# Fourteen zero stores cut from 128 rows to 120, and one more of 112 rows

## The chip, the cores and the metric

The kernel runs on one core of a Trainium2 chip. The metric is the device time of one execution in microseconds (us). The core has a tensor engine (PE, with its weight loads shown as PEld), a vector engine (DVE), a scalar engine (ACT), GpSimd (POOL) and a sync engine (SP). Here SP issues nearly all transfers between the chip's memory (DRAM) and the on-chip memory (SBUF, 128 rows called partitions). The transfers are carried by 16 DMA engines, which the profile counts together.

## The reference

A decoder of four layers runs forward and backward for a single token of 1,024 numbers: attention, MLP, attention, MLP, both times with the same weights. Cut to what matters:

```python
def A(x, k_cache, v_cache, wq, wo):          # attention over the last W = 4096 keys of 32768
    q = x @ wq                               # 32 heads of 128
    k, v = k_cache[:, :, Sk - W:], v_cache[:, :, Sk - W:]    # 4 groups
    p = softmax(q @ k.T * Dh ** -0.5)
    return (p @ v) @ wo
def B(x, w1, b1, w2):                        # 1024 -> 3584 -> 1024
    h = x @ w1 + b1
    return (h * tanh(softplus(h))) @ w2
x = x + A(norm(x), ...); x = x + B(norm(x), ...); x = x + A(norm(x), ...); x = x + B(norm(x), ...)
out, vjp = jax.vjp(f, x, k_cache, v_cache, wq, wo, w1, b1, w2)
return out, *vjp(grad_out)
```

The outputs are the result and the gradients of all eight inputs in bfloat16. The gradients of `k_cache` and `v_cache` have the caches' full size, 4 groups x 32,768 keys x 128; only the last 4,096 keys of each group were read, so the first 28,672 rows of each group are zero. Writing these zeros is part of the result: 8 areas of 7.3 MB, 58.7 MB out of the 168 MB that the SP queue moves.

## The kernel before

All matrices pass through SBUF in tiles of 128 partitions. The forward and backward pass work layer by layer: attention forward (`attn_fwd`, layer A1), the MLP forward with a first part of its backward (`mlp_B2_fwd`), attention again (A3), the last MLP forward and backward (`mlp_B4`), then `attn_bwd` for A3, `mlp_B2_bwd`, and `attn_bwd` for A1. The last part makes the weight gradients, which are outer products: `run_jobs` goes through a list of jobs (w2, then w1 mixed with the K and V gradients, then wo and wq), each of which multiplies on PE, moves the product from PSUM to SBUF with ACT or DVE (L890 and L893), and stores it.

The order of the work is written out by hand; there is no scheduler. SP issues its transfers strictly in program order. The transfers rotate over eight completion semaphores (101 to 106, 109 and 110), so that a transfer is issued only when the one eight before it has landed. Loads of weights stand in a list, `queue`, and `pump` (L182, L190, L199, L201) issues the next one when its slot of a ring is given back.

The zeros are cut into 112 jobs, `zero_jobs`: two outputs x 4 groups x 14 pieces. An area is seen as 128 rows of 57,344 bytes (`zflat`), and a piece is 2,048 elements of every row, so 128 x 4,096 bytes. `zeros(n)` takes the next n jobs and issues a store for each (two adjoining ones go in one store where the source has 4,096 elements). The source changes over the program: `zlo`, 1,024 elements read twice (L149); `zt`, 2,048 elements (L151); at the end `z8`, 4,096 elements (L151). Calls of `zeros` are spread over the whole program: in `attn_fwd` by the list `Z_`, in `mlp_B4` by `ZB4` after each block, in `attn_bwd`, in `mlp_B2_bwd`, and from `out_step` and `run_jobs` on beside the outer products. There is no wait for a zero store other than the semaphore rotation and the reuse of its source.

The names that matter below: `zero_jobs`, `zeros`, `zsrc` (the present source and its width), `Z_`, `ZB4`, `run_jobs`, and `add("w2", ...)`, whose last argument is the number of zero stores that follow a job of w2.

Of the kernel before, what the change touches and what calls it, by code (L numbers as in the profile page):

```python
# [17 lines left out]
G = 4  # L18
# [3 lines left out]
def kernel(  # L22
# [22 lines left out]
    nc = tc.nc  # L45
# [8 lines left out]
    ZR = Sk - W  # L54
# [33 lines left out]
    sB, sA, zlo, zt = misc[:, 0:1024], misc[:, 1024:2048], misc[:, 2048:3072], misc[:, 1024:3072]  # L88
# [42 lines left out]
    zero_jobs = []  # L131
    per = ZR // P * DH
    for out_t in (out_2, out_3):
        for g in range(G):
            zflat = out_t[0, g, 0:ZR, :].rearrange("(p r) d -> p (r d)", p=P)
            for i in range(per // 2048):
                zero_jobs.append((zflat, i))
    zsrc = [None, 1024]

    def zeros(n, after=None):  # L140
        while n > 0 and zero_jobs:
            zf, i = zero_jobs.pop(0)
            k = 1
            if zsrc[1] == 4096 and n > 1 and zero_jobs and zero_jobs[0][1] == i + 1 and i % 2 == 0:
                zero_jobs.pop(0)
                k = 2
            dst = zf[:, i * 2048:(i + k) * 2048]
            if zsrc[1] == 1024:
                d = nc.sync.dma_start(dst.rearrange("p (a b) -> p a b", a=2), zlo[:, None, :].to_broadcast([P, 2, 1024]))  # L149
            else:  # L150
                d = nc.sync.dma_start(dst, zsrc[0][:, 0:k * 2048])  # L151
            gate(d, after)
            after = None
            n -= k
# [301 lines left out]
    def attn_fwd(x_col, l, first, p_dst, F_, Z_):  # L456
        sv, n_bf, g0 = ln_fwd(x_col, l)
        if first:
            constants()
        zeros(Z_[0])  # L460
        big = two_banks()
        for t in range(TD):
            for n in range(8):
# [73 lines left out]
        nc.vector.tensor_copy(operm[:], pps[:])  # L537
        o32 = kt([P, HQ], FP32, f"o32_{l}")
        nc.vector.tensor_copy(o32[:], acc[:])
        zeros(Z_[2])  # L540
        sv["o32"], sv["p"] = o32, p_dst
        fill(F_[4])
        R = one_tile("R", 512)
# [84 lines left out]
            nc.vector.tensor_mul(d3[:, 1, :], dps[:], m3[:, 1, :])  # L628

    def mlp_B2_fwd(x_col):  # L630
        zeros(3)
        sv, n_bf, g0 = ln_fwd(x_col, "B2")
        hacc = one_tile("acc", TF)
        for i in range(16):
            t, hf = i // 2, i % 2
            w, ring, sl = take(("w1h", i))
            for b in range(NW2):
                fb = hf * NW2 + b
                o = (b // 2) * 2 * P + b % 2
                mm(hacc[:, fb:fb + 1], w[:, o:o + 2 * P - 1:2], n_bf[:, t:t + 1], i == 0 and b == 0, t == TD - 1)  # L640
            rel(ring, sl)
            if i == 1:
                bcast_g(gpair[:, LI["B4"], :])
        zeros(1)
        h = wk("h", TF)
        nc.vector.tensor_add(h[:], hacc[:], b1_f[:])
        dact = kt([P, TF], FP32, "dact_B2")
        mish(h[:], apair[:, 1, :], dact[:], TF)
        sv["dact"] = dact
        R, dps, ds = w2_pass(apair[:, 1, :], gpair[:, LI["B4"], :], {8: 1, 9: 1, 10: 1, 11: 1})  # L650
        nc.gpsimd.memset(sA, 0.0)
        zsrc[:] = [zt, 2048]
        da4 = kt([P, TF], FP32, "da4")
        y = d_cols(R)
        x_new = kt([P, TD], FP32, "x_B2")
        nc.vector.tensor_add(x_new[:], x_col[:], y[:])
        da_merge(da4[:], dps, ds)
        return x_new, sv, da4

    def mlp_B4(x_col, da4):  # L660
        sv, n_bf, g0 = ln_fwd(x_col, "B4", 2)
        dh = kt([P, TF], FP32, "dh_B4")
        sv["dh"] = dh
        R = one_tile("R", 512)
        big = two_banks()
        blk, hcol = {}, {}

        def fwd(b):
            full = b < 3
            nh, nt, nch = (2, 2, 4) if full else (1, 4, 2)  # L670
            hb = big[b % 2]
            blk[b] = [take(("w1b", b, i)) for i in range(nch)]
            for i in range(nch):
                fill(FT4[b][i])
                w = blk[b][i][0]
                for ti in range(nt):
                    t = nt * i + ti
                    for n in range(nh):
                        g = 2 * n + ti if full else ti
                        mm(hb[32 * g:32 * g + 32, :], bc(n_bf[:, t:t + 1]), w[:, ti, n * 512:(n + 1) * 512],  # L680
                           i == 0, i == nch - 1, tile_position=(0, 32 * g))
            evac(jkf[:, :], hb[:], 512, "D")

        def sel(b):
            full = b < 3
            nh, nk = (2, 8) if full else (1, 4)
            hps = sm_tile(P, 8)
            for cc in range(2):
                for tt in range(2):
                    k = 2 * cc + tt  # L690
                    mm(hps[:, k:k + 4 * (nh - 1) + 1:4], jkf[:, cc * 256 + tt:cc * 256 + tt + 255:2], selD[:] if full else sel1[:], k == 0, k == 3)
            h = wk("h", nk)
            nc.vector.tensor_add(h[:], hps[:, 0:nk], b1_f[:, 8 * b:8 * b + nk])
            hcol[b] = h

        def act(b):
            nk, f0 = 8 if b < 3 else 4, 8 * b
            dact = wk("dact", nk)
            mish(hcol[b][:], apair[:, 0, f0:f0 + nk], dact[:], nk)
            nc.vector.tensor_mul(hpair[:, 0, f0:f0 + nk], da4[:, f0:f0 + nk], dact[:])  # L700
            nc.vector.tensor_mul(dh[:, f0:f0 + nk], da4[:, f0:f0 + nk], dact[:])
            spent(2.8, 0.2)

        def turn(b, lo, hi):
            for u in range(lo, hi):
                if b < 3:
                    w = blk[b][u // 2][0][:, u % 2, :]
                    T8([w[:, (k // 2) * 256 + k % 2:(k // 2) * 256 + k % 2 + 255:2] for k in range(8)], w)
                else:
                    w = blk[b][u // 2][0][:, 2 * (u % 2):2 * (u % 2) + 2, :]  # L710
                    T8([w[:, q, (k // 2) * 256 + k % 2:(k // 2) * 256 + k % 2 + 255:2] for q in range(2) for k in range(4)],
                       w.rearrange("p t f -> p (t f)"))

        def bwd(b):
            nk, f0 = 8 if b < 3 else 4, 8 * b
            for k in range(nk):
                for tp in range(4):
                    w = blk[b][tp][0][:, 0:2, :] if b < 3 else blk[b][tp // 2][0][:, 2 * (tp % 2):2 * (tp % 2) + 2, :]
                    mm(R[32 * tp:32 * tp + 32, 0:256].rearrange("p (t d) -> p t d", t=2), bc(hpair[:, 0, f0 + k:f0 + k + 1]),
                       w[:, :, k * P:(k + 1) * P], b == 0 and k == 0, b == 3 and k == nk - 1, tile_position=(0, 32 * tp))  # L720
            for _, ring, i in blk.pop(b):
                rel(ring, i)

        for b in range(4):
            fwd(b)
            fill(FB4[b][0])
            sel(b)
            act(b)
            turn(b, 0, 8 if b < 3 else 4)
            fill(FB4[b][1])  # L730
            bwd(b)
            if b == 3:
                zsrc[:] = [None, 1024]
            zeros(ZB4[b])
        evac(jkf[:, 0:256], R[:, 0:256], 256, "D")
        dn = sm_tile(P, TD)
        for i in range(2):
            mm(dn[:].rearrange("p (a i) -> p i a", i=2)[:, i, :], jkf[:, i * P:(i + 1) * P], ident_f[:, 0:P:32], i == 0, i == 1)
        tt = wk("xx", 2 * TD)
        nc.vector.tensor_copy(tt[:, 0:TD], dn[:])  # L740
        return tt, sv

    def attn_bwd(g_col, g_bf, l, sv, last, nxt, F_, Z_, step):
# [9 lines left out]
            nc.gpsimd.dma_start(wo[:, 0, :], p3_d[:])  # L753
        else:
            p_t, ds_t = sv["p"], sA
        zeros(Z_[0])
        acc = one_tile("acc", HQ)
        j_cols(big, acc, 8, F_[0], True)
        do32 = wk("do32", HQ)
# [32 lines left out]
            rings["rb"] += range(2, 8)  # L792
            pump()
        nc.scalar.activation(dqpair[:, LI[l], :], qacc[:], ACT.Copy, scale=scale)
        zeros(Z_[2])
        step(3)
        fill_kind("wq")
        R = one_tile("R", 512)
# [229 lines left out]
    def wo_dead():  # L1028
# [32 lines left out]
        after = []  # L1061
# [9 lines left out]

        for n in range(NW2 // 2):
            add("w2a", n, lambda c=2 * n: pair_half(row_sp["w2"], c, w2_out, w2_lhs, 0))
            add("w2", n, lambda c=2 * n: pair_half(row_sp["w2"], c, w2_out, w2_lhs, 1), 1)
        for n in range(16):
            add("w1", n, lambda t=n // 2, hf=n % 2: w1_job(t, hf))
            add("kv", n, lambda n=n: kv_step(n))
# [5 lines left out]
    def run_jobs(n):  # L1083
        while jobs and (n > 0 or not jobs[0][0]):
            job, f, z = jobs.pop(0)
            f()
            zeros(z)
            n -= job

    def kv_step(i):  # L1090
# [13 lines left out]
    def out_step(i):  # L1104
        if i == 0:
            nc.scalar.copy(z8.bitcast(FP32), zlo[:, 0:2].bitcast(FP32).to_broadcast([P, 2048]))
            zsrc[:] = [z8, 4096]
            zeros(8)
        elif i < 3:
            rows_turn(row_sp["w2"], i - 1, w2_sp[i - 1], "rep")  # L1110
        elif i > 2:
            run_jobs(1 if i == 4 else 2)

    ZB4 = [11, 11, 10, 8]
    FT4 = [(0, 0, 0, 0), (6, 2, 2, 2), (6, 2, 2, 2), (8, 3)]
    FB4 = [(1, 0), (1, 0), (1, 0), (1, 2)]

# [5 lines left out]
    g3, g3b, _ = ln_bwd(tt, sB4, gcol, "A3", nfill=2)  # L1123
    g2, g2b, _ = attn_bwd(g3, g3b, "A3", sA3, False, "B2", [4, 3, 5, 2], [5, 1, 5], lambda i: None)
    (g1, g1b, _), x4_bf = mlp_B2_bwd(g2, g2b, sB2, x3)
    zeros(4)
    g0, g0b, _ = attn_bwd(g1, g1b, "A1", sA1, True, "X0", [0] * 4, [0, 0, 0], out_step)
    assert not queue and not held and not units
    order[:] = ["op", "lo", "hi", "op", "acc", "R", "op", "sm"]
# [3 lines left out]
    p_l.extend([sA3["p"], sA1["p"]])  # L1133
    ds_l.extend([sA3["ds"], sA1["ds"]])
    run_jobs(1000)
    assert not zero_jobs


# [28 lines left out]
```

## Time and profile before

| | |
|---|---|
| time, median of 3 runs | 438.72 us (436.29 to 438.74) |
| the profiled execution | 439.71 us, span 437.9 us |
| busy PE, DVE, ACT | 322.9, 234.0, 219.2 us |
| moved by DMA | 169.98 MB, mean 388 GB/s |
| read from DRAM, written to it | 70.27 MB, 99.10 MB |
| zero stores from `misc` (`zlo`, `zt`) | 97 of 512 KB, median 10.3 us from issue to landing |

The span is the time from the first to the last instruction that the profile holds; the execution's own time has 1.8 us around it. "Busy" is the time in which an engine has an instruction under way. The profile cuts the span into 40 equal slices and gives the busy share of each in tenths; its DMA row is the mean over the 16 DMA engines. For each transfer the trace holds the issue, the packets (one for each piece of a row; start, duration and size, without the engine's number), and 16 landing marks, one from each DMA engine.

### The profile page before, as it was taken

The page shows a single profiled execution, that of the slowest core. Times are in us where ns is not written, and L with a number is a line of the kernel's source. Part 1 is how long each engine was busy: PE and PEld are TensorE (multiplying, and loading weights), DVE is VectorE, ACT ScalarE, POOL GpSimd, SP SyncE. Part 2 cuts the span into 40 slices and gives each one's busy share as a digit, 9 for nine tenths or more (in the row PEclk, how much of TensorE's full clock was granted, in tenths as well). Part 3 has the DMA queues.
Part 4 walks back from the last instruction along what each step waited for, and adds up shares of the span by engine and source line. Part 5 has one row for each costly group of instructions (what it writes and reads, how often), then busy time and mean ns, then how long its engine had stood idle before and what let it go on. Part 6 is the DMA issues. An engine that isn't in the chain of part 4 may idle for free.

```text
span 437.9 us, 9216 instructions
## 1 busy us (share of the span) xinstructions
PE 322.9 (74%) x3732; PEld 189.0 (43%) x3732; DVE 234.0 (53%) x532; ACT 219.2 (50%) x335; POOL 15.4 (4%) x54
## 2 busy tenths in 40 slices
PE   3475746477788878588789749767889799999830
PEld 1164315355365666477567427755423123321100
DVE  2035102088364456255565548664266999899940
ACT  1036000046273456356445236464467689899950
POOL 2000000000000000000000000000400020000000
PEclk9999555569898999889999877686875555555555
DMA  8999999999999999998999998999999999999995
GB/s 334 422 420 416 412 409 388 392 378 359 392 414 405 418 328 392 398 416 265 413 410 404 380 413 286 377 370 352 409 423 418 419 414 412 403 402 411 410 412 229
DMA packets 50215, 169.98 MB, mean 388 GB/s; under 512 B 4832, under 2 KB 5884, under 8 KB 46076
## 3 DMA queue, kind: packets, MB, share of 16 engines
q1 hardware_dynamic: 49696, 168.32, 98.2%
q0 software_dynamic: 416, 1.06, 0.6%
q8 instruction: 29, 0.48, 0.4%
q14 instruction: 14, 0.11, 0.1%
q10 hardware_dynamic: 60, 0.01, 0.0%
HBM read 70.27 MB, written 99.10 MB: 387 GB/s over the span
## 4 chain that ended last, share of the span: by engine, by line
PE 18%; DMA 17%; ACT 8%; DVE 4%; issue 2%; SPq 1%; ACTq 0%; DVEq 0%
DMA out_dram<-misc 8%; DMA K<-in_B_w_dram 7%; PE op L238 4%; ACT wo L893 4%; PE R L238 3%; ACT wq L893 2%; PE acc L238 2%; DMA out_dram<-wo 2%; PE sm L238 2%; PE tp L258 2%; ACT K L231 2%; PE lo L238 2%; PE hi L238 1%; PE tp L924 1%; DVE wo L890 1%
## 5 line engine op out<-in xcount | busy, mean ns | idle before, releaser
L231 ACT COPY K<-tp 128x1024 bf16<-128x1024 bf16 x59 | 57.9, 1015 | 22.7 <-PE tp L258 22.1
L258 PE MATMUL tp<-ident_bf,K 128*128 128x128 bf16 x656 | 52.7, 239 | 8.4 <-ACT K L231 3.4
L238 PE MATMUL op<-wo 2*128 2x512 bf16 (+2 forms) x123 | 52.0, 559 | 5.0 <-ACT wo L893 2.7
L231 ACT COPY wo<-tp 128x1024 bf16<-128x1024 bf16 x33 | 33.5, 1023 | 36.3 <-PE tp L258 33.6
L258 PEld LDWEIGHTS <-K 128*128 128x128 bf16 x656 | 44.3, 108 | 16.0 <-issue 11.4
L238 PEld LDWEIGHTS <-wo 128*128 128x128 bf16 (+2 forms) x590 | 24.3, 101 | 62.2 <-issue 53.3
L893 ACT CAST wo<-op 128x512 bf16<-128x512 f32 (+1 forms) x51 | 31.4, 631 | 8.0 <-PE hi L238 2.2
L590 DVE CUSTOM_DVE_ANT_0 K<-K,kp 128x1024 bf16<-128x1024 bf16 (+1 forms) x22 | 24.6, 1127 | 12.5 <-PE R L238 8.8
L258 PE MATMUL tp<-ident_bf,wo 128*128 128x128 bf16 x336 | 26.4, 235 | 0.3 <-ACT wo L231 0.3
L229 DVE COPY jk<-R 128x512 f32<-128x512 f32 (+1 forms) x11 | 7.3, 665 | 34.3 <-PE R L238 34.3
L258 PEld LDWEIGHTS <-wo 128*128 128x128 bf16 x336 | 21.5, 106 | 7.7 <-issue 7.6
L238 PE MATMUL acc<-wo 2*128 2x512 bf16 (+1 forms) x41 | 24.1, 588 | 0.2 <-DVE V L890 0.2
L238 PE MATMUL lo<-wo 2*128 2x512 bf16 x41 | 24.1, 588 | 0.0
L238 PE MATMUL hi<-wo 2*128 2x512 bf16 x41 | 24.0, 586 | 0.0
L229 DVE COPY wo<-tp 128x1024 bf16<-128x1024 bf16 x19 | 12.8, 688 | 16.8 <-PE tp L258 16.8
L238 PE MATMUL sm<-wo 2*128 2x512 bf16 (+1 forms) x33 | 19.8, 600 | 1.3 <-DVE cols L378 1.3
L231 ACT CAST jk<-hi 128x512 bf16<-128x512 f32 x4 | 2.6, 659 | 35.9 <-PE hi L238 35.9
L229 DVE COPY K<-tp 128x1024 bf16<-128x1024 bf16 x23 | 15.6, 689 | 9.1 <-PE tp L258 9.0
L890 DVE CAST wo<-op 128x512 bf16<-128x512 f32 (+1 forms) x32 | 18.4, 598 | 3.7 <-DMA out_dram<-wo 2.3
L238 PE MATMUL R<-wo 2*128 2x512 bf16 (+1 forms) x33 | 19.6, 593 | 0.6 <-DVE wo L890 0.4
L231 ACT COPY wq<-tp 128x1024 bf16<-128x1024 bf16 x14 | 14.1, 1014 | 11.2 <-PE tp L258 8.4
L229 DVE CAST jk<-lo 128x512 bf16<-128x512 f32 x4 | 2.8, 712 | 30.3 <-PE lo L238 30.3
(295 smaller groups left out, 643.0 us busy)
## 6 DMA issues: line engine op xcount, KB each, us to landing
out_dram<-misc SPq DMA_DIRECT2D x97, 512.0 KB, 10.3
out_dram<-wo SPq DMA_DIRECT2D x39, 512.0 KB, 9.5
K<-in_B_w_dram SPq DMA_DIRECT2D x28, 512.0 KB, 10.0
K<-in_A_k_cache_dram SPq DMA_DIRECT2D x9, 1024.0 KB, 15.6
wq<-in_A_wq_dram SPq DMA_DIRECT2D x8, 1024.0 KB, 10.1
out_dram<-wq SPq DMA_DIRECT2D x8, 1024.0 KB, 12.6
K<-in_B_w_dram SPq DMA_DIRECT2D x16, 448.0 KB, 5.8
out_dram<-wo SPq DMA_DIRECT2D x16, 448.0 KB, 7.8
```

The lines of the kernel that those rows point to most:

```text
L229: return nc.vector.tensor_copy(out_ap, in_ap)
L231: return nc.scalar.copy(out_ap, in_ap)
L238: return nc.tensor.matmul(out_ap, lhsT=lhsT, rhs=rhs, start=start, stop=stop, skip_group_check=True, **kw)
L258: nc.tensor.transpose(ps[:, b * P:(b + 1) * P], ap, ident_bf[:])
L590: return nc.vector.tensor_tensor_reduce(out=w, in0=w, in1=vec, scale=1.0, scalar=0.0, op0=ALU.mult, op1=ALU.add, accum_out=acc_col)
L890: nc.vector.tensor_copy(out_ap, in_ap)
L893: nc.scalar.copy(out_ap, in_ap)
L924: nc.tensor.transpose(ps[:, j * P:(j + 1) * P], spread_t[:, j, :], ident_bf[:])
```

## The change

The 14 pieces of the last area (the last group of `out_3`) are taken off `zero_jobs` and put in a list of their own, `part`. Fourteen stores write only the first 120 of the 128 rows of a piece; a fifteenth writes what is left of the area, its last 1,792 rows of 128 elements, as 112 rows of 4,096 bytes. `part_zeros(n)` issues the next n of them, and the calls of `zeros` over the program give some of their number to it, with the source that is valid there. `zeros(3)` in `mlp_B2_fwd` becomes `zeros(2, parts=1)`, and so on. `ZB4[1]` goes from 11 to 12, of which one is short, so one full store more stands there. In the last part, `out_step` issues two short stores and then six full jobs, the w2 job 3 is followed by a short store, and the w2 job 5 by the one of 112 rows. The bytes written are the same. All stores stay on the SP queue.

```diff
@@ -136,8 +136,25 @@
     zsrc = [None, 1024]
-
-    def zeros(n, after=None):
+    part = [(zero_jobs[-1][0], i, 120) for i in range(per // 2048)]
+    part.append((part[0][0], 0, 8))
+    del zero_jobs[-(per // 2048):]
+
+    def part_zeros(n):
+        for _ in range(n):
+            zf, i, rows = part.pop(0)
+            if rows == 120:
+                dst = zf[0:120, i * 2048:(i + 1) * 2048]
+            else:
+                rows = 112
+                dst = out_3[0, G - 1, ZR - ZR // 16:ZR, :].rearrange("(p r) d -> p (r d)", p=112)
+            if zsrc[1] == 1024:
+                nc.sync.dma_start(dst.rearrange("p (a b) -> p a b", a=2), zlo[0:rows, None, :].to_broadcast([rows, 2, 1024]))
+            else:
+                nc.sync.dma_start(dst, zsrc[0][0:rows, 0:2048])
+
+    def zeros(n, after=None, parts=0):
+        part_zeros(parts)
         while n > 0 and zero_jobs:
...
     def attn_fwd(x_col, l, first, p_dst, F_, Z_):
-        zeros(Z_[0])
+        zeros(max(Z_[0] - 1, 0), parts=Z_[0] > 0)
...
-        zeros(Z_[2])
+        zeros(max(Z_[2] - 2, 0), parts=2 * (Z_[2] > 0))
...
     def mlp_B2_fwd(x_col):
-        zeros(3)
+        zeros(2, parts=1)
...
-            zeros(ZB4[b])
+            zeros(ZB4[b] - 1, parts=1)
...
     def attn_bwd(g_col, g_bf, l, sv, last, nxt, F_, Z_, step):
-        zeros(Z_[0])
+        zeros(max(Z_[0] - 1, 0), parts=Z_[0] > 0)
...
-        zeros(Z_[2])
+        zeros(max(Z_[2] - 1, 0), parts=Z_[2] > 0)
...
-            add("w2", n, lambda c=2 * n: pair_half(row_sp["w2"], c, w2_out, w2_lhs, 1), 1)
+            add("w2", n, lambda c=2 * n: pair_half(row_sp["w2"], c, w2_out, w2_lhs, 1), 2 if n in (3, 5) else 1)
...
     def run_jobs(n):
             f()
-            zeros(z)
+            if z > 1:
+                part_zeros(z - 1)
+            else:
+                zeros(z)
...
     def out_step(i):
-            zeros(8)
+            zeros(6, parts=2)
...
-    ZB4 = [11, 11, 10, 8]
+    ZB4 = [11, 12, 10, 8]
...
-    zeros(4)
+    zeros(3, parts=1)
```

More of the change, by code (lines that the diff above doesn't have):

```diff
@@ L1135 @@
     run_jobs(1000)
-    assert not zero_jobs
+    assert not zero_jobs and not part
 _INS = ['A_x', 'A_k_cache', 'A_v_cache', 'A_wq', 'A_wo', 'B_x', 'B_w1', 'B_b1', 'B_w2', 'grad_out']
```

## The prediction

> **What bounds the kernel now.** I read the busy table first, then the 40 slices, the DMA queues, three stretches of the span, the issues of the SP queue, and last the landings in the trace. The page:
>
> ```profile
> PE 322.9 (74%) x3732; PEld 189.0 (43%) x3732; DVE 234.0 (53%) x532; ACT 219.2 (50%) x335; POOL 15.4 (4%) x54
> ...
> DMA  8999999999999999998999998999999999999995
> ...
> q1 hardware_dynamic: 49696, 168.32, 98.2%
> ...
> q8 instruction: 29, 0.48, 0.4%
> ```
>
> No compute engine reaches 75%. The DMA row is 9 in nearly every slice, and the SP queue alone (q1) holds the sixteen DMA engines for 98.2% of the span. So bytes and the engines that carry them set the time. The stretches (span, busy of PE, PEld, DVE, ACT, POOL, clock, DMA share, GB/s) say where it is so:
>
> ```profile
> 200.00:202.00 2.00, 1.79 (x33) 1.67 (x31) 0.69 (x1) 1.60 (x2) 0.00 (x0) 1.00 0.45 120
> 202.00:262.00 60.00, 46.51 (x708) 34.43 (x705) 32.68 (x77) 27.44 (x31) 1.45 (x3) 0.94 1.02 392
> 262.00:312.00 50.00, 40.29 (x530) 29.39 (x534) 29.85 (x67) 26.77 (x28) 2.06 (x4) 0.73 0.98 355
> 312.00:421.00 109.00, 97.91 (x600) 28.93 (x588) 92.50 (x175) 92.36 (x182) 7.32 (x35) 0.55 1.02 412
> 421.00:431.00 10.00, 0.00 (x0) 0.00 (x0) 0.25 (x1) 0.66 (x2) 0.00 (x0) 0.50 1.02 414
> 431.00:437.90 6.90, 0.00 (x0) 0.00 (x0) 0.00 (x0) 0.00 (x0) 0.00 (x0) 0.50 0.28 116
> ```
>
> A share of 1.02 is a full engine, since packet records overlap by 3 ns. At 200 us the transfers run nearly dry (0.45). From 312 us they do not, and the last 17 us have no compute at all: stores drain. In the timeline the last issue is
>
> ```profile
> 420.89 2.27 SPq L1001 DMA_DIRECT2D out_dram<-wq  x2
> ```
>
> The question is whether all engines drain together. Each SP transfer makes 16 landing marks in the trace, one for each engine. For the last store thirteen fall between 432.87 and 433.18, then one each at 433.79, 434.15 and 436.85; the span ends at 437.9, 1.1 us after the last. One engine is 2.7 us behind the next and 3.8 us behind the pack, and its lateness is the end of the kernel.
>
> That lag grows steadily: the gap between the last two marks of a store is 0.62 us for the store that lands at 337.9, 1.69 us at 360.9, 2.7 us from 400 on. The packet records fit. Between 342 and 360 us, 1,311 of 1,372 packets of 4,096 bytes took 159 ns and the other 61 on average 169; of those of 3,584 bytes 473 of 509 took 140 ns. About one packet in nineteen, close to one engine's sixteenth, is 6% slow, and 6% of the 23 us between those two stores is 1.4 us, against the 1.07 us that the gap grew. The second and third marks have another source: an instruction fetch (q8, 29 packets, 1,000 ns on average) holds one engine at a time.
>
> [...]
>
> **The change part by part.**
>
> *Removed from one engine.* A 128-row store gives each engine eight packets of 4,096 bytes (or sixteen of 2,048). Fourteen stores lose eight rows; if that is one engine's share, it is rid of 14 x 8 = 112 packets. The 112-row store returns 7 to every engine: net -105 there (105 x 0.169 = 17.7 us), +7 on the other fifteen (7 x 0.159 = 1.1 us).
>
> *Where they lie.* From the order on the SP queue: eleven short stores and one more full store stand before the last out-product part (which starts near 312 us), three short stores and the 112-row one in it. In the last part a fully used engine goes from 15 x 8 = 120 zero packets to 11 x 8 + 3 x 8 + 7 = 119: -0.16 us. The spared engine goes to 11 x 8 + 7 = 95: -25 packets, -4.2 us, more than its 2.7 us gap. If it is the slow one, the end passes to the second mark, 434.15: -2.7 - 0.16 = **-2.9 us**. This is the main term; the last 17 us hold no compute that could hide it.
>
> *Before the last part.* The added full store (eight packets, 1.27 us, before 200 us) lies where the engines otherwise run dry: 0.55 x 2 = 1.1 us idle, so +0.2 us. In the DMA-bound stretch from 202 to 262 us three short stores spare the slow engine 3 x 8 x 0.169 = 4.1 us; loads of w2 there land at 251.68 with their sixteenth mark and 251.11 with the fifteenth, and at 267.03 against 266.37, which PE waits for. That is at most -0.66 us; I take half, -0.3, since the stretch after it is mostly PE's (40.3 of 50 us). Other landings that compute waits for (296.56 against 295.25) are late by an instruction fetch that the change does not touch: 0.
>
> *Issue and waits.* Two more transfers (292 for 290: the 112-row one, and one pair of 4,096-element stores falls apart). An SP issue takes some 0.4 us (the first two in the trace 0.38 and 0.42), and SP's longest waits are for PE and for landings:
>
> ```profile
> SPq L182 <- PE acc L238: 40.1, 41, 6.4
> SPq L182 <- PE R L238: 21.3, 5, 8.0
> SPq L151 <- DMA out_dram<-misc: 21.0, 25, 1.4
> ```
>
> Eight semaphores rotate, so a transfer waits for the eighth before it; a short store takes a slot like a full one, and loads of w1, w2 and K stand behind it in the same order. Cover if it failed: 2 x 0.4 = 0.8 us. I take 0. No wait, tile or compute instruction is added.
>
> *The unknown: the speed of a short store.* In the kernel before every SP transfer has 128 rows, so no row shows a store whose rows are split by fifteen. Lower bound: 159 ns a packet, as now, 0 us. [...] Below 0 there is nothing to gain: 159 ns is what nearly all packets take beside fifteen others. I take 0, by the nearest row, the 159 ns: the marks of one store lie 0.3 to 2 us apart, so the engines seldom do the same place of a store at once.
>
> Sum: 439.71 (the profiled execution; its span of 437.9 and 1.8 around it) - 2.9 + 0.2 - 0.3 = 436.7. The median of the runs, 438.72, is 1.0 under the profiled one, so **435.7 us**, 0.7% faster. Full balance (all marks at 433.0) would give 1 us more.
>
> **The rivals.**
>
> [...]
> [...]
>
> *The wrong engine is spared.* Nothing in the trace numbers the slow engine. If another one is slow, it does 119 packets in the last part for 120 (-0.16) and the extra full store earlier (+0.2, at worst +1.3): 438.6 to 440, say 438.9. For: fifteen others. [...]
> [...]
>
> *It does not run on fifteen engines.* If 120 rows go to eight engines or to all sixteen, a short store makes 15 packets on eight (about +1.1 us each, part of it evened out, near 443) or spares nobody (438.9).
>
> **How the numbers follow.** Forecast 0.47 (433.5 to 437.5), shared ports 0.28 (437 to 455), wrong engine 0.20 (438.6 to 440), not fifteen 0.05. One per cent, 4.4 us, is about what a measurement of this kernel tells from no change. Below 434.3: a quarter of the forecast case, where the loads in the middle give more than I took, 0.12. Above 443.1: two thirds of the ports case and half of the last, 0.21. Between: 0.67. The range, 433.2 to 446.0, leaves out the far ports case (about 0.12) and a few hundredths below. The forecast's own range stands above.
>
> **What would show it.** In the profile after: the landing marks of the last store within some 1.4 us instead of 4, with the last at about 434; fifteen marks for each 120-row store; packets of the short stores at 159 ns. [...] Wrong engine: one mark still 2.7 us late at the end. The prediction is wrong if the lag at the end is unchanged, if short stores land slower, or if the lag turns out to be that of the profiled execution alone.

## The result and the profile after

The changed kernel takes 443.61 us (median of 6, 440.75 to 447.58) against 438.57 us (median of 6, 436.29 to 439.75) for the kernel before in the same comparison: ratio 1.0119, 95% interval 1.0077 to 1.0161. It is slower by 5.0 us (5.2 by the ratio), where 3 us less were forecast, and the interval lies wholly above 1.

One of the six runs (447.58 us) was in a slower state: the ratios here and below leave such runs out, the medians keep them, and the profile shown is of another execution of the changed kernel, with a span of 444.4 us (446.21 us in all). It is called "the changed kernel" below. Its page:

```profile
PE 325.6 (73%) x3732; PEld 191.0 (43%) x3732; DVE 234.2 (53%) x532; ACT 219.3 (49%) x335; POOL 15.4 (3%) x54
...
DMA  8999999999999999899999998999999999999996
...
q1 hardware_dynamic: 49802, 168.32, 97.8%
...
q8 instruction: 29, 0.48, 0.4%
```

The compute engines have nearly the same busy times as before, and SP's queue still holds the DMA engines for 97.8% of the span. But the span of this execution is 6.5 us longer than that of before, so the same 168.32 MB keep the engines busy for longer: 0.978 x 444.4 = 434.6 us per engine, against 0.982 x 437.9 = 430.0. Of the 6.5 us, 4.6 are slower transfers and 1.9 idle time.

The same kernel cut into stretches (span, busy of PE, PEld, DVE, ACT, POOL, clock, DMA share, GB/s), first through to the drain, then the issues at the end and SP's waits:

```profile
200.00:202.00 2.00, 1.55 (x35) 0.94 (x32) 1.03 (x2) 0.41 (x1) 0.00 (x0) 1.00 1.03 420
202.00:262.00 60.00, 49.62 (x743) 37.09 (x738) 33.63 (x78) 29.05 (x32) 1.45 (x3) 0.94 1.03 387
262.00:312.00 50.00, 38.36 (x490) 29.56 (x494) 28.46 (x63) 24.95 (x26) 0.00 (x0) 0.66 0.97 359
312.00:427.00 115.00, 101.30 (x636) 30.17 (x628) 92.88 (x177) 93.29 (x181) 9.40 (x37) 0.56 1.01 396
427.00:437.00 10.00, 0.39 (x1) 0.00 (x0) 1.31 (x3) 1.72 (x4) 0.00 (x0) 0.50 1.02 417
437.00:444.40 7.40, 0.00 (x0) 0.00 (x0) 0.00 (x0) 0.00 (x0) 0.00 (x0) 0.50 0.45 185
```

```profile
427.75 2.47 SPq L1018 DMA_DIRECT2D out_dram<-wq  x2
```

```profile
SPq L199 <- PE acc L255: 38.6, 41, 6.0
SPq L199 <- PE R L255: 16.4, 5, 6.3
SPq L168 <- DMA out_dram<-misc: 9.5, 18, 1.1
```

In the last part the share of 1.01 is a full engine as before, and the rate fell from 412 to 396 GB/s. From 427 us on, where only drained stores of full shape are left, it is 417 again. SP's waits for PE became no longer (38.6 and 16.4 us, for 40.1 and 21.3 before). The last issue moved from 420.89 to 427.75, and the last landing mark from 436.85 to 443.44.

The loss is not only in the last part. Summing rate times length from 312 us to the end gives 49.9 MB before and 51.1 MB after: at 312 us the changed kernel is 1.2 MB behind, 3.0 us at 410 GB/s. The other 3.5 us of the 6.5 are lost later.

A lone short store shows it best. The store of 120 rows issued at 341.10 us has its eighth landing mark at 347.43 us, the one of 112 rows issued at 351.52 at 355.82. Around them, the stretches of the changed kernel:

```profile
337.00:342.00 5.00, 4.96 (x30) 0.82 (x28) 3.92 (x7) 4.42 (x9) 0.00 (x0) 0.50 1.02 409
342.00:347.00 5.00, 4.57 (x24) 2.85 (x24) 3.63 (x11) 2.58 (x5) 0.00 (x0) 0.50 1.00 349
347.00:351.00 4.00, 1.50 (x10) 0.23 (x10) 2.41 (x11) 1.83 (x4) 0.00 (x0) 0.50 0.97 363
351.00:356.00 5.00, 3.97 (x23) 0.85 (x22) 4.90 (x10) 4.12 (x9) 0.00 (x0) 0.50 0.94 334
356.00:361.00 5.00, 4.70 (x30) 1.46 (x29) 4.54 (x12) 3.65 (x9) 3.01 (x11) 0.50 0.96 363
```

and of the kernel before, where the same place holds stores of 128 rows only:

```profile
342.00:347.00 5.00, 3.09 (x22) 0.50 (x19) 4.80 (x15) 3.59 (x8) 0.00 (x0) 0.50 1.03 419
347.00:352.00 5.00, 4.26 (x28) 1.25 (x28) 4.71 (x13) 3.50 (x8) 1.53 (x3) 0.50 1.03 419
```

From 342 to 347 us the engines are nearly as busy (1.00 for 1.03) and carry 349 GB/s in place of 419. The packet records say how: of the 4,096-byte packets that start there, 0 of 512 took over 215 ns before; in the changed kernel 49 of 426 did, 32 of them 215 to 350 ns and 17 longer, while the median stayed at 159 ns. The landing marks say what it costs: the eighth mark of successive stores comes at 345.21, 347.43 (the short one), 348.69 and 349.95 us, 2.22 us for the short store against 1.26 for a full one. (One of the short store's sixteen marks comes early, at 342.50 us, so its eighth mark is that of the seventh engine with data.) The last mark, on which the end of the kernel hangs, loses too: 349.64, 352.16 and 353.41 us, 2.52 us for the short store against 1.25 for the next.

### The profile page after: what moved, and what is told of

Read it like the earlier page. It is cut to its first block, busy times and chain, and to the rows that moved or that the text cites. A ratio compares the mean times of both kernels' runs of the same rounds, so it can differ in the third digit from the quotient of the medians.

```text
span 445.8 us, 9218 instructions
## 1 busy us (share of the span) xinstructions
PE 328.0 (74%) x3732; PEld 193.9 (43%) x3732; DVE 234.3 (53%) x532; ACT 219.5 (49%) x335; POOL 15.4 (3%) x54
## 3 DMA queue, kind: packets, MB, share of 16 engines
q1 hardware_dynamic: 49802, 168.32, 97.2%
## 4 chain that ended last, share of the span: by engine, by line
PE 19%; DMA 18%; ACT 8%; DVE 5%; issue 2%; ACTq 0%; SPq 0%; DVEq 0%
DMA out_dram<-wo 7%; DMA K<-in_B_w_dram 7%; DMA out_dram<-misc 5%; PE tp L275 4%; ACT wo L910 4%; PE R L255 3%; ACT wq L910 2%; PE acc L255 2%; PE op L255 2%; PE sm L255 2%; ACT K L248 2%; PE lo L255 1%; PE hi L255 1%; DVE wo L907 1%; DVE V L907 1%
## 5 line engine op out<-in xcount | busy, mean ns | idle before, releaser
L275 PE MATMUL tp<-ident_bf,K 128*128 128x128 bf16 x656 | 55.0, 246 | 8.0 <-DMA K<-in_B_w_dram 3.0
L275 PEld LDWEIGHTS <-K 128*128 128x128 bf16 x656 | 46.6, 112 | 15.3 <-issue 10.5
```

The lines of the kernel that those rows point to most:

```text
L275: nc.tensor.transpose(ps[:, b * P:(b + 1) * P], ap, ident_bf[:])
```

## The experiments

All comparisons are with the kernel before, run on the same chip. Diffs are against the changed kernel, and `...` marks what is left out, unless said otherwise. The table gathers the results; "slowed packets" are the 4,096-byte packets of 215 to 350 ns in one profiled execution. "Engines used" is fifteen for the forms of store that left fifteen marks as data landed (seen in the changed kernel and in "four apart, 15"), and is taken as sixteen for the others.

| kernel | rows of a short store | engines used | median us | ratio (95%) | slowed packets |
|---|---|---|---|---|---|
| before | 128 | 16 | 438.6 to 439.2 | 1 | 118 |
| changed, again | 120 in a run | 15 | 446.73 | 1.0162 (1.0085 to 1.0239) | 327 |
| full rows | 128 | 16 | 437.83 | 0.9992 (0.9953 to 1.0030) | 100 |
| 112 rows | 112 in a run | 16 | 444.74 | 1.0130 (1.0052 to 1.0208) | 278 |
| nine apart | 0, 9, ... 126 | 15 | 443.90 | 1.0137 (1.0044 to 1.0229) | 200 |
| flat | 120 in a run | 15 | 443.21 | 1.0096 (1.0055 to 1.0137) | 246 |
| four apart, 15 | 32, 36, ... 88 | 15 | 438.54 | 1.0004 (0.9972 to 1.0035) | 132 |
| eight apart | 0, 8, ... 120 | 16 | 447.60 | 1.0185 (1.0136 to 1.0233) | 446 |
| four apart, 16 | 32, 36, ... 92 | 16 | 437.85 | 0.9983 (0.9959 to 1.0008) | 114 |
| late short | 120, last part only | 15 | 439.75 | 1.0022 (0.9991 to 1.0053) | 175 |
| early short | 120, before it only | 15 | 439.83 | 1.0039 (1.0009 to 1.0069) | 162 |

### Is it the place of the stores or their shape?

Full rows at the same places: the order of the changed kernel, but each of the fourteen stores has 128 rows and the store of 112 rows falls away.

```diff
-    part = [(zero_jobs[-1][0], i, 120) for i in range(per // 2048)]
+    part = [(zero_jobs[-1][0], i, 128) for i in range(per // 2048)]
...
-            if rows == 120:
-                dst = zf[0:120, i * 2048:(i + 1) * 2048]
+            if rows == 0:
+                continue
+            dst = zf[0:rows, i * 2048:(i + 1) * 2048]
```

> The changed kernel with its fourteen short stores made full again (128 rows, at the places where the change put them) and the 112-row store left out; the same bytes as the kernel before. It keeps the new order of the zero stores and takes away the split by fifteen. [...] Placement (the full store moved ahead of 200 us, fewer zeros in the last part): the loss stays, ratio 1.008 to 1.016. [...]

Measured: 437.83 us, 0.9992. The place, the order on the queue and the added store before 200 us cost nothing that can be measured; the shape costs all of it. (In this kernel the added store is a full one. In the changed kernel it is a short one: at `ZB4[1]` eleven full stores and a short one stand in place of eleven full ones.)

The changed kernel again, on the same chip as the others:

> The changed kernel itself once more, for a profile to set beside the others and a time on the same chip. Ratio 1.008 to 1.016. [...] Wrong engine: the last mark of the last store is again more than 2 us behind the one before it.

Measured: 446.73 us, 1.0162; its interval and the first one, 1.0077 to 1.0161, overlap widely.

112 rows, with two stores of 112 rows for what remains. The changed kernel's own store of 112 rows left sixteen marks as data landed and none early (354.71 to 361.91 us in its profile of 445.8 us), so no engine is spared; the even share of each is seven rows in place of eight:

```diff
-    part = [(zero_jobs[-1][0], i, 120) for i in range(per // 2048)]
+    part = [(zero_jobs[-1][0], i, 112) for i in range(per // 2048)]
...
-            if rows == 120:
-                dst = zf[0:120, i * 2048:(i + 1) * 2048]
+            if rows == 112:
+                dst = zf[0:112, i * 2048:(i + 1) * 2048]
```

> The fourteen short stores have 112 rows instead of 120 (seven rows for each of sixteen engines) and two stores of 112 rows write the rest. [...] Wrong engine or fifteen engines as such: no loss from the split, ratio 0.998 to 1.004.

Measured: 444.74 us, 1.0130. It takes no engine away and loses as much. In its last part the rate falls with the share still full:

```profile
343.00:348.00 5.00, 1.93 (x13) 0.51 (x13) 3.21 (x13) 2.45 (x5) 0.00 (x0) 0.50 1.01 376
348.00:353.00 5.00, 4.09 (x23) 0.79 (x22) 4.90 (x12) 3.50 (x8) 0.00 (x0) 0.50 1.01 348
```

So the loss is not that one engine fewer carries the data, nor an uneven split. What both shapes may share is that an engine reads other rows than in a store of 128 rows. The records don't name the engine or the row of a packet, so the next kernels test it.

### Which rows does an engine have to read?

The zeros of the last area are all alike, so a store may read them from any row of the source. The next kernels use this. "Flat" is their control: the area is cut lengthwise into pieces of 120 x 4,096 bytes, and the source rows stay 0 to 119.

```diff
-                nc.sync.dma_start(dst, zsrc[0][0:rows, 0:2048])
+                nc.sync.dma_start(flat.rearrange("(e x) d -> e (x d)", e=k), zsrc[0][0:k, 0:2048])
```

> The control for the run with rows of their own: the same lengthwise cut of the area, but the source is again 120 (112) rows one after the other. [...] If the lengthwise cut of the destination were what matters: ratio as in the run with own rows.

Measured: 443.21 us, 1.0096. The cut of the destination in DRAM is not what matters.

Nine apart: fifteen single rows, 0, 9, ... 126, are read eight times each.

```diff
+                nc.sync.dma_start(flat.rearrange("(e r x) d -> e r (x d)", e=k, r=8),
+                                  zsrc[0][0:9 * k - 8:9, None, 0:2048].to_broadcast([k, 8, 2048]))
```

> [...] The pieces are cut from the area lengthwise so that each engine writes 32 KB in a run. [...] Fifteen engines as such, whatever rows they read: the loss stays, ratio 1.008 to 1.016.

Measured: 443.90 us, 1.0137: fifteen single rows still lose. (The rest goes out from fourteen rows.) The slowed packets fell only to 200, in the fastest of its four runs. Full stores stand on both sides of each short one in the queue, and the first and the last mark of a store near 341 us are 2.8 us apart in the profile of before, more than one store's 1.26 us, so some engines could read the full store while others read the short one. The author supposed that the choice of rows then matters, and took other ones; which engine reads which row no run shows.

Four apart, fifteen engines: the same store with the rows 32, 36, ... 88. The rest goes out from the sixteen rows 32 to 92 in the same way.

```diff
+            k, r = (16, 7) if rows == 8 else (15, 8)
...
+                nc.sync.dma_start(flat.rearrange("(e r x) d -> e r (x d)", e=k, r=r),
+                                  zsrc[0][32:32 + 4 * k - 3:4, None, 0:2048].to_broadcast([k, r, 2048]))
```

> [...] The rest goes out on sixteen engines, seven packets each, from rows 32 to 92. [...] Fifteen engines as such: ratio 1.008 to 1.016. If the spared engine is the slow one, the last mark of the last store stands within 1.5 us of the pack; if not, 2.5 us or more behind it.

Measured: 438.54 us, 1.0004. The loss is gone with fifteen engines still in use. Its stretches round the same lone short store, whose eighth mark is here at 340.00 us:

```profile
330.00:335.00 5.00, 4.75 (x35) 0.92 (x32) 3.79 (x7) 4.22 (x9) 0.00 (x0) 0.50 1.02 414
335.00:340.00 5.00, 4.64 (x25) 2.81 (x24) 4.16 (x11) 3.23 (x7) 0.00 (x0) 0.50 1.01 411
340.00:344.00 4.00, 2.51 (x15) 0.47 (x17) 3.89 (x13) 2.96 (x6) 0.00 (x0) 0.50 1.02 415
```

411 GB/s at the short store, with 414 and 415 on either side: no dip. The eighth marks before, of and after it come at 338.72, 340.00 and 341.24 us.

A pair in one comparison on sixteen engines: the rows 0, 8, ... 120, eight apart, and as a control 32, 36, ... 92, four apart. Both write fourteen full pieces.

```diff
-            if rows == 120:
+            if rows == 8:
+                continue
...
+                                  zsrc[0][0:121:8, None, 0:2048].to_broadcast([16, 8, 2048]))
```

> Fourteen full pieces on sixteen engines, at the places of the change and without a rest, but each engine reads its eight packets from one row: 0, 8, 16, ... 120. [...] Nothing is spared and no row is odd. [...] If fifteen engines as such or short stores cost the time: ratio 0.997 to 1.003.

> [...]

Measured: 447.60 us (1.0185) with rows eight apart, 437.85 us (0.9983) with rows four apart. The same packets on sixteen engines, with nothing but the source rows changed, are 2.0% apart by the ratios, some 9 us. The kernel with rows eight apart, round the store issued at 344.4 us:

```profile
342.00:347.00 5.00, 4.89 (x31) 1.80 (x27) 3.17 (x5) 3.69 (x7) 0.00 (x0) 0.50 1.02 410
347.00:352.00 5.00, 3.86 (x18) 1.81 (x19) 4.66 (x14) 3.31 (x7) 0.00 (x0) 0.50 1.02 319
352.00:357.00 5.00, 3.96 (x25) 0.70 (x24) 4.22 (x12) 2.83 (x6) 0.00 (x0) 0.50 1.01 383
```

That the choice of rows alone makes the loss is shown by this pair. How the rows make it is not shown. The rows 0, 8, ... 120 and the rows 0, 9, ... 126 both lose, and their intervals, 1.0136 to 1.0233 and 1.0044 to 1.0229, don't tell the two apart. Nor was every packet slowed: 446 were and 211 took longer still (118 and 114 before), where nine of the fourteen stores alone hold 1,152 packets of 4,096 bytes.

### Where in the program is it lost?

Two halves of "flat": short stores only in the last part (three), or only before it (eleven). The rest of the area goes out from the rows 32, 36, ... 92 in one store. The diff is against "flat", of the late half; the early one has `i < 11`.

```diff
-            k = 112 if rows == 8 else 120
+            short = i > 10
...
+            k = 120 if short else 128
```

> Flat cut as in the kernel with consecutive rows, but only the three stores of the last part (after 312 us) have 120 rows; the eleven before it have 128, and what is left goes out in one small store of one row per engine (rows 32 + 4e, 6,144 bytes each). Theory that every short store costs some 0.3 us of the end wherever it stands (4.5 us over fifteen): 1 us, ratio 1.001 to 1.004. Theory that the loss of the pack at a short store in the last part, 0.85 to 0.9 us at each lone one or pair, is paid in full at the end: 1.75 us, ratio 1.003 to 1.006. Rival that the early ones are absorbed where the queue runs dry and the last part carries the whole loss: ratio 1.008 to 1.012.

> The other half: the eleven stores before the last part have 120 rows, the three in it 128, and the rest goes out in one store of one row per engine (four packets of 5,632 bytes on each). Theory that the loss is spread over all of them: 3 us, ratio 1.005 to 1.009. Rival that the early ones are absorbed: ratio 0.998 to 1.002. Together with the late half the two losses should add to the 1.0096 that all fifteen cost in the flat cut; a sum far from it would mean that one hides the other.

Measured: late 1.0022 (0.9991 to 1.0053), early 1.0039 (1.0009 to 1.0069). The sum of the two losses, 1.0061, is under the 1.0096 of "flat", but within the intervals; the two halves hold fourteen of its fifteen short stores, and the one of 112 rows is in neither. The rival that the early ones are absorbed and the last part carries the whole loss (1.008 to 1.012 for the late half) is out. Whether the late ones cost 0.3 us each or their whole dip of nearly 1 us, the other two cases expected, the interval doesn't tell. The early half is below the 1.005 to 1.009 expected, though not outside it by the interval. Worked out per store it is 0.32 us for the three late ones (0.0022 x 439.2 / 3) and 0.16 us for the eleven early ones (0.0039 x 439.2 / 11), with intervals that overlap.

### Which engine is the slow one?

The forecast hung on the engine that is last at the end. "Four apart, 15" tests it, since there the sparing costs nothing that can be measured (1.0004). In its store of 120 rows, issued at 334.5 us, fourteen marks fall at 339.43 to 341.45 and a fifteenth at 342.52; the late mark is one of the fifteen. In the full store two later there is one early mark at 340.63, the next at 342.02: the spared engine, 1.4 us ahead of the pack. The last store's marks run from 431.12 to 431.52, then 432.41 and 434.86: the last one is still 2.45 us behind. So in this execution the engine that a split by fifteen leaves out was not the slow one; it was in the pack and is now ahead of it, to no use. The changed kernel shows the same: the late mark of 352.16 us is one of the fifteen of its short store, 2.5 us behind the one before.

Two kernels looked for its number with small stores in the last part, on the first k engines alone. A small store whose marks hold the late one has the slow engine below k. This takes it that each store uses the same engines in the same order, which the marks don't name. The first cut the last piece into sixteen stores of 8, 7, 15, 14, 12, ... rows (diff against the kernel before):

```diff
+    probes = [8, 7, 15, 14, 12, 10, 9, 11, 13, 6, 5, 4, 3, 2, 1, 8]
...
+            if job and probes:
+                probe()
```

> The kernel before, with its last zero piece cut into sixteen small stores of 8, 7, 15, 14, 12, 10, 9, 11, 13, 6, 5, 4, 3, 2, 1 and 8 rows, one after each of the first sixteen jobs of the last part. A store of k rows makes k marks from engines. The slow engine is late by more than 1 us in the full stores beside them. [...] If another engine is slow, its late mark is in the 15-row store and vanishes at some smaller number, which gives its place. Time: up to 4 us over the kernel before, for sixteen more slots in the rotation of eight.

Measured: 442.39 us, one run, and no answer. Each small store took one of the eight places in the rotation, the queue ran shallow (the full stores among them landed 4.3 us after their issue in the median, for 9.3 in the kernel before), and the lag of the last mark in them was at most 0.54 us, so there was no late mark to look for. It did show that a store of k rows, k under 16, gives k marks as data land, and one about 1 us after its issue.

The second read the rows 32, 36, ... in eight stores with two packets from each row (one where k is 16), one after every second job of w1:

```diff
+    probes = [8, 12, 4, 14, 6, 10, 2, 16]
...
+        nc.sync.dma_start(out_3[0, G - 1, lo:lo + 16 * k * r, :].rearrange("(e r x) d -> e r (x d)", e=k, r=r),
+                          zsrc[0][32:32 + 4 * k - 3:4, None, 0:2048].to_broadcast([k, r, 2048]))
```

> The kernel before, but of its last area thirteen pieces are full 128-row stores cut lengthwise and the fourteenth is cut into eight small stores, one after every second w1 job (350 to 400 us). They use one row per engine, 32 + 4e, two packets on each of the first 8, 12, 4, 14, 6, 10, 2 engines and one packet on 16. Looked for: the slow engine's number. Full stores near the probes should have their last mark 1.5 to 2.5 us behind the second last. A probe on the first k engines shows such a late mark only if the slow engine's number is below k. Theory that the slow engine is number 14: the late mark is in the probe of 16 alone, and the probe of 14 is tight (within 0.7 us). Rival, a lower number n: the late mark is in every probe with k above n, so that the smallest k with it and the largest without it enclose n. If the probes again drain the queue and the lag falls below 0.7 us in the full stores beside them, the place stays open. [...]

Measured: the gap between the last two marks of each small store, and of a full store next to it:

```
k                 8     12    4     14    6     | 10    2     16
small store, us   1.37  1.41  0.25  1.79  1.98  | 0.01  0.04  0.03
full store, us    1.67  1.37  1.91  1.83  1.98  | 0.64  0.66  0.04
```

The first five enclose it: late at 8, 12, 14 and 6, not at 4. If the stores do use the engines in one order, the slow engine of this execution was the fifth or the sixth of it, number 4 or 5 counted from 0. The last three tell nothing of it: from 374 us the queue had run dry, the lag began anew and stayed small, and the 0.64 us of the full store beside the store of 10 is in none of that store's marks, so it is another engine's. With that number, and that order, the engine can't be spared by a split by fewer than sixteen: leaving out number 4 or 5 would also leave out all above it.

Its time was a miss, 449.06 us (one run) against 439.58 for the kernel before (one run). The stretches and POOL's timeline, here and then in the kernel before, show why:

```profile
350.00:374.00 24.00, 20.17 (x119) 5.91 (x118) 20.99 (x46) 19.86 (x40) 2.66 (x9) 0.50 1.00 397
374.00:400.00 26.00, 16.34 (x99) 5.52 (x100) 13.96 (x24) 13.88 (x29) 1.78 (x8) 0.50 0.61 241
400.00:440.00 40.00, 28.82 (x115) 5.97 (x112) 31.78 (x53) 32.95 (x68) 0.00 (x0) 0.50 1.02 411
```

```profile
378.96 0.73 POOL L916 COPY wo<-gpair 128x32 bf16<-128x32 bf16 x2 [25.44 <-DMA out_dram<-wo]
```

```profile
367.27 0.47 POOL L903 COPY wo<-npair 128x32 bf16<-128x32 bf16 x2 [13.80 <-PE tp L924]
```

From 374 to 400 us the DMA share is 0.61: 0.41 x 26 = 10.7 us are idle. POOL spreads the operands of a later job into the tile `wo`, and the source of the zeros is another part of that tile. In the kernel before these copies wait for PE at the most. Here the first one waits on five semaphores, those of the five small stores issued before it, the last of which landed at 378.73, and the next two copies each wait for one more small store; PE, DVE, ACT and so SP stood behind them. That is a cost of the small stores, not of the rows.

## Why the prediction was wrong

The forecast was 435.7 us, the measured time 443.6. Two steps failed, and both failures are among the rivals, which were given their chances as if only one of the cases could come.

**"The unknown: the speed of a short store ... I take 0."** This step made the sign wrong. The argument was that the marks of one store lie 0.3 to 2 us apart, so that engines seldom do the same place of a store at once. But the distance of two marks (near 341 us it is 2.8 us from the first to the last) says nothing of the rows that the engines read at one moment, and being out of step did not prevent the loss. Measured: 0.96 us more for the lone short store of the last part, at the eighth mark, and 0.34 us on the time for each of the fifteen ((443.61 - 438.57) / 15). The kernels with 112 rows, with rows eight apart and with rows four apart show that it is the rows: 1.0130, 1.0185 and 1.0004. The nearest row was the wrong one to choose, since no row of before has another split at all.

**"If it is the slow one, the end passes to the second mark ... -2.9 us."** The main term never came. With rows four apart, where sparing costs nothing, the time is 1.0004 of before and the last mark still 2.45 us late: the spared engine was not the slow one in that execution, nor in the changed kernel's, where the last mark is 2.05 us late at the end. The lag itself is a poorer base than it looked. At the end it is 2.70 us in the profile of before, but 1.43 with full rows, 1.43 with rows four apart on sixteen engines and 0.72 in "flat". The reading "one engine is 6% slow" holds for a time only: in the profile of before some 4% of the 4,096-byte packets took 161 to 180 ns from 320 to 360 us, but 58% from 420 us on, and the gap is 2.66 us for the store that lands at 397 us and 2.70 for the last. The lag is gained mostly in the first part of that stretch (2.46 us for the store that lands at 378.5) and then carried along.

**The terms that held.** Place and order, +0.2, and issue, 0: the kernel with full rows at the same places measures 0.9992, so their sum is within 0.5% of nothing. The extra place before 200 us where the queue ran nearly dry is not a fixed one: in the changed kernel 200 to 202 us has a share of 1.03. The -0.3 for the loads of w2 needed the slow engine to be spared and falls with the main term; from 202 to 262 us the changed kernel issues four short stores, not three (at 204.98, 218.15, 230.46 and 248.89). The cover for the issues was priced too low: 0.4 us is what the first ones take, while in the profile of before the last two take 2.27 us together. That the kernel is bound by its DMA engines was right, and it is why a slowed packet shows in the time at all.

**The rivals.** *Shared ports*, at a chance of 0.28 and 437 to 455 us, has the measured 443.6 in its range. But no run shows that engines share a port, and the times and chances put on that case were the author's estimate. What the runs showed in its place is that the rows read decide (1.0185 against 0.9983); the fifteen stores cost 5.0 us. *The wrong engine* came true as well: the last mark stayed late. Its price of 438.9 us was short by 4.7, since the loss by the rows came on top. *Not fifteen engines* is out: the short store at 341 us has one mark at 342.50, and fifteen from 346.65 to 352.16.

**What was to show it.** The last mark was still late, by 2.05 us, as named for the wrong engine, and packets did not stay at 159 ns: 327 of 215 to 350 ns in the changed kernel for 118 before. Whether they were on all engines the records don't tell.

What stays open: whether number 4 or 5 is the slow one in other executions, why the lag stops growing, how the choice of rows makes the loss, within a store or with the stores beside it, and why the rows 0, 9, ... 126 lose as much as a plain split. No kernel tried here is faster than the one before by more than these runs can tell; the best, sixteen rows four apart, is at 0.9983 (0.9959 to 1.0008).

## What to carry to other kernels

In a kernel bound by its DMA engines, as this one is, keep the stores from SBUF at 128 rows, or measure another choice of rows before it is relied on: here fifteen stores with rows in a run, fourteen of 120 and one of 112, came out at 1.0096 to 1.0162, and sixteen of 112 at 1.0130. When the source may be any row (a constant), the rows 32, 36, ... up to 88 or 92 cost nothing that these runs can tell, with fifteen engines (1.0004) or with sixteen (0.9983). Before work is taken from "the late engine", prove its number with small nested stores that leave the queue full and whose source no later copy has to wait for, and price two rivals that don't exclude each other together as well as alone.

## What the runs showed of the hardware

- A busy DMA queue can be a slow one: a share of 1.00 went with 349 GB/s where one of 1.03 had gone with 419. The rate, not the share, showed the loss.
- The dip of one 480 KB store is 0.96 us at the eighth mark and 1.27 us at the last, where a full store takes 1.26 us.
- Which rows fifteen engines read decided the time: 1.0137 with rows 0, 9, ... 126, against 1.0004 with rows 32, 36, ... 88.
- A store of k rows with k under 16 left k + 1 marks: one early and k as data land (9, 13, 5, 15, 7, 11 and 3 marks for k of 8, 12, 4, 14, 6, 10 and 2).
- A few small stores can empty the queue: through POOL's waits for their landing the DMA share fell to 0.61 over 26 us.
